# Backward of two linear-attention and two sliding-window layers: attention backward in 24 visits a chunk, weights transposed on TensorE, a set order for the forward's DMA queue, and later clearing of the ring

## The chip, the cores and the metric

The kernel runs on one core of a Trainium2 chip. TensorE (PE; its weight loads are shown apart as PEld), VectorE (DVE), ScalarE (ACT), GpSimd (POOL) and SyncE (SP, which only issues DMAs here) run side by side, each through its own instructions in order, and meet at semaphores. TensorE writes to PSUM alone, which has eight banks of 2 KB a partition. The metric is the time of one launch on the device in microseconds. Before: 2201.24 us, the median of three runs (2200.07 to 2201.99).

## The reference

Four residual blocks are applied to a sequence of 2048 rows of 640 columns in bfloat16: linear attention (weights A), sliding-window attention (weights B), then both once more with the same weights. The kernel returns the output, the gradient of the input, and the gradients of the four weight matrices, each summed over the two layers that share it.

```python
def _A_ref(x, wqkv, wo):                       # 32 heads of 20
    q, k, v = split(x @ wqkv)
    phi = lambda t: jnp.where(t > 0, t + 1, jnp.exp(t)) + 1e-6
    pq, pk = phi(q), phi(k)
    kv = jnp.einsum("bhsd,bhse->bhde", pk, v)
    z = jnp.einsum("bhsd->bhd", pk)
    o = jnp.einsum("bhqd,bhde->bhqe", pq, kv) / (jnp.einsum("bhqd,bhd->bhq", pq, z)[..., None] + 1e-6)
    return merge(o) @ wo
def _B_ref(x, wqkv, wo):                       # a window of 256 keys, causal
    q, k, v = split(x @ wqkv)
    scores = jnp.einsum("bhqd,bhkd->bhqk", q, k) * (20 ** -0.5)
    mask = (i - j >= 0) & (i - j < 256)
    p = softmax(jnp.where(mask, scores, -1e9))
    return merge(jnp.einsum("bhqk,bhkd->bhqd", p, v)) @ wo
x = x + _A_ref(layernorm(x), Aw, Ao);  x = x + _B_ref(layernorm(x), Bw, Bo)
x = x + _A_ref(layernorm(x), Aw, Ao);  x = x + _B_ref(layernorm(x), Bw, Bo)
_out, _vjp = jax.vjp(_f, A_x, A_wqkv, A_wo, B_wqkv, B_wo); grads = _vjp(grad_out)
```

With tiles of 128 rows there are 16 of them, and a window of 256 keys reaches over at most three tiles of keys: the query's own (masked on the diagonal), the one before it, and the one before that (masked the other way).

## The kernel before, in words

**Order of the work.** All is emitted by `passes` (L1268 on). (1) `forward`: a first pass over the 16 tiles for layer 0's features and their sums, then layers 0 and 1 together, tile by tile, then layers 2 and 3. (2) `core` for layer 3: the attention backward. (3) layer 2's linear backward. (4) `core` for layer 1. (5) layer 0's linear backward, with weight-gradient products between its steps, and then the rest of the weight gradients.

**Plans.** Each stage is a list of pairs (place, function). A place is a number of plan steps; the functions are emitted in the order of their places. The places stand in the table `PLACES` (L41). Four engines (PE, DVE, ACT, POOL) keep the order in which the code emits: `run` opens a `manual_schedule` with these four. The order of SP's queue, which issues every DMA, is left to a scheduler. `forward` has 430 plan steps before its end: the first pass has six steps a tile, the later layers eight (`B1`, `B3` are the first steps of the second and third part).

**Forward.** For a tile of layers 1 and 3, `qkv` writes q, k and v to a ring tile `s` (128 rows, 3 x 32 heads padded to 32 columns); two DMA transposes make its turned copy `T`; both are stored, 768 KB each, for the backward. The five ring tiles' padding is set at the very start, by three POOL memsets a tile (L284 to L286). `plan_scores` forms scores for four (head group, key tile) blocks in one visit: 16 matmuls on 32 rows, one `exp` of 128 x 2048 on ACT, masks on POOL; `b_pv` applies them to the values. Layer norm's reciprocal root is a POOL power (L424).

**Attention backward (`core`, `core_steps`, `core_step`, `core_acc`).** A chunk `c` is two query tiles. It is taken in four quarters of eight heads (two groups of four); each quarter loads its slabs (`core_loads`): q, k, v turned, and q and k as they are, for k and v over all four key tiles. A visit is one group, one query tile and two of the four heads: 32 visits a chunk. The visits are pipelined. In the step of visit n, PE forms the gradient scores `dp` of visit n-3 and the scores `s` of visit n (32-row matmuls on four row groups, one PSUM buffer of two banks for each), ACT makes `e = exp(s)`, DVE the product `ds = dp * e`, POOL masks `e`, and `ds` of an earlier visit is turned to `dsT`. Then comes a piece of the plan (norm backward, projections of the neighbouring chunks), and `core_acc` sums visit n-7 into two banks: 128 x 128 matmuls of 20 columns, from `ds`, `e` and `dsT`.

`dsT` is made in one of two ways. From the third chunk on, `by_dma` (table `bd`) sends 13 of 32 visits to a DMA transpose; the others are transposed by PE (L700) and copied by ACT (L705) or DVE (L707). Which of the two copies, and how many filler transposes PE gets (`thin`; six and four a visit in the first two chunks), is worked out by a small model of the engines' loads in `core`, corrected by table `xx`. After each group the banks are emptied: L753 keeps half of one for the next chunk, L757 adds that half, L759 scales the query gradient.

**Weights.** The backward needs each weight turned. `core`'s hooks of layer 3 load them by seven DMA transposes (`turned`), Wo of B is turned on PE near the end of the forward (`turn_wo`), and two are parked in memory for layer 1.

## Time and profile before

The profile shows one execution on the chip; the sequencers' own waits and issues are not counted as busy.

| what | value |
|---|---|
| median of the runs | 2201.24 us |
| the profiled execution, its span | 2199.58 us, 2197.9 us |
| granted TensorE clock, mean | 0.984 |
| busy: PE, DVE, ACT, POOL | 93 %, 63 %, 61 %, 49 % |
| DMA | 453.26 MB in 708193 packets, mean 206 GB/s |
| first and last `ds` of layer 3's backward | 659.8 us and 1091 us |
| first and last `ds` of layer 1's backward | 1261 us and 1690.7 us |

A row of the groups reads: line, engine, operation, what is written and from what, its shape, the count, then busy time and mean length of one in ns, then the idle time of the engine before it and what ended most of it. Matmuls overlap and their ends are modelled, so a matmul's length is longer than the distance from one to the next; that distance is told by the starts.

### The profile page before, as it was taken

The page shows a single profiled execution, that of the slowest core. Times are in us where ns is not written, and L with a number is a line of the kernel's source. Part 1 is how long each engine was busy: PE and PEld are TensorE (multiplying, and loading weights), DVE is VectorE, ACT ScalarE, POOL GpSimd, SP SyncE. Part 2 cuts the span into 40 slices and gives each one's busy share as a digit, 9 for nine tenths or more (in the row PEclk, how much of TensorE's full clock was granted, in tenths as well). Part 3 has the DMA queues.
Part 4 walks back from the last instruction along what each step waited for, and adds up shares of the span by engine and source line. Part 5 has one row for each costly group of instructions (what it writes and reads, how often), then busy time and mean ns, then how long its engine had stood idle before and what let it go on. Part 6 is the DMA issues. An engine that isn't in the chain of part 4 may idle for free. (4 is left out here: it accounts for less than half of the span.)

```text
span 2197.9 us, 74336 instructions
## 1 busy us (share of the span) xinstructions
PE 2041.3 (93%) x30981; PEld 1586.3 (72%) x30981; DVE 1390.2 (63%) x2840; ACT 1342.4 (61%) x2009; POOL 1083.0 (49%) x1887
## 2 busy tenths in 40 slices
PE   7989998899989999998879899999988899999999
PEld 5667776577767877777768687777776788888644
DVE  6788886888836887887748668888876233320000
ACT  5468886388876887887637677888876233330000
POOL 2046665166675577777534456777764312220000
PEclk9999999999999999999999999999999999999999
DMA  7498885799979499998799734999987999998650
GB/s 258 146 253 229 237 233 146 171 234 245 232 218 255 111 200 198 210 206 192 157 293 275 198 106 115 197 208 202 210 189 165 271 307 246 266 228 241 220 162 21
DMA packets 708193, 453.26 MB, mean 206 GB/s; under 512 B 419728, under 2 KB 684688, under 8 KB 707472
## 3 DMA queue, kind: packets, MB, share of 16 engines
q1 hardware_dynamic: 707856, 448.51, 81.2%
q8 instruction: 242, 3.96, 0.8%
q14 instruction: 95, 0.78, 0.1%
HBM read 213.09 MB, written 149.82 MB: 165 GB/s over the span
## 5 line engine op out<-in xcount | busy, mean ns | idle before, releaser
L680 DVE TENSOR_TENSOR ds<-dp,e 128x768 bf16<-128x768 f32 (+2 forms) x512 | 464.0, 906 | 173.8 <-PE s L138 55.6
L677 ACT ACTIVATE e<-s 128x768 bf16<-128x768 f32 (+2 forms) x512 | 395.7, 773 | 137.5 <-PE s L138 110.4
L383 ACT ACTIVATE eT<-sT 128x2048 bf16<-128x2048 f32 x180 | 338.0, 1878 | 89.0 <-PE sT L138 85.2
L138 PE MATMUL wg<-rhs,lhs 128*128 128x240 bf16 (+3 forms) x2880 | 372.2, 286 | 7.7 <-DMA lhs<-o 7.7
L138 PEld LDWEIGHTS <-lhs 128*128 128x128 bf16 x2880 | 262.1, 98 | 97.2 <-DMA lhs<-o 9.6
L689 POOL TENSOR_SCALAR_AFFINE_SELECT e<-e 128x256 bf16<-128x256 bf16 x512 | 207.2, 406 | 249.8 <-ACT e L677 246.9
L138 PEld LDWEIGHTS <-dqT 128*128 128x128 bf16 x1920 | 171.8, 98 | 62.2 <-issue 10.4
L391 POOL TENSOR_SCALAR_AFFINE_SELECT eT<-eT 128x512 bf16<-128x512 bf16 x256 | 165.5, 650 | 98.7 <-ACT eT L383 98.7
L138 PE MATMUL acc<-slabqs,ds 128*128 128x20 bf16 x2880 | 210.0, 172 | 1.4 <-ACT dq L759 0.5
L138 PE MATMUL dp<-slabvT,dT 32*128 32x384 bf16 (+2 forms) x1024 | 168.0, 320 | 44.3 <-DVE ds L680 39.6
L138 PE MATMUL acc<-ds,e 128*128 128x20 bf16 x2880 | 208.0, 171 | 0.0
L138 PEld LDWEIGHTS <-ds 128*128 128x128 bf16 x2880 | 187.9, 96 | 11.7 <-issue 3.5
L693 POOL TENSOR_SCALAR_AFFINE_SELECT e<-e 128x256 bf16<-128x256 bf16 x448 | 194.9, 435 | 0.0
L138 PEld LDWEIGHTS <-e 128*128 128x128 bf16 x2880 | 170.0, 96 | 10.6 <-issue 1.8
L1140 DVE CAST wr<-wg 128x240 bf16<-128x240 f32 (+3 forms) x54 | 24.4, 452 | 240.1 <-PE wg L138 228.8
L700 PE MATMUL flip<-ident,ds 128*128 128x128 bf16 x1944 | 169.7, 221 | 3.3 <-DVE ds L787 1.2
L138 PE MATMUL s<-slabkT,slabqT 32*128 32x384 bf16 (+2 forms) x1024 | 167.9, 323 | 4.1 <-ACT e L677 3.5
L1138 ACT CAST wr<-wg 128x240 bf16<-128x240 f32 (+3 forms) x36 | 14.3, 397 | 245.9 <-PE wg L138 241.3
L1033 POOL TENSOR_TENSOR dh<-dh,lg 128x640 f32<-128x640 f32 x32 | 46.0, 1437 | 238.1 <-DVE s L1030 235.1
L138 PE MATMUL dense<-WTA,dqT 128*128 128x320 bf16 x960 | 162.6, 301 | 0.6 <-DVE dqT L1007 0.3
L138 PE MATMUL dense<-WB,hnT 128*128 128x320 bf16 x960 | 160.1, 301 | 0.4 <-DVE s L500 0.3
L138 PE MATMUL acc<-slabks,dsT 128*128 128x20 bf16 x2880 | 147.3, 171 | 14.0 <-DMA dsT<-ds 13.0
(175 smaller groups left out, 4483.0 us busy)
## 6 DMA issues: line engine op xcount, KB each, us to landing
s<-s SPq DMA_DIRECT2D x32, 768.0 KB, 4.1
T<-T SPq DMA_DIRECT2D x32, 768.0 KB, 3.9
dqkv<-dq SPq DMA_DIRECT2D x16, 960.0 KB, 5.6
dqkv<-dqa SPq DMA_DIRECT2D x32, 480.0 KB, 5.1
rhs<-dqkv SPq DMA_DIRECT2D x32, 480.0 KB, 5.4
rhs<-dqkv SPq DMA_DIRECT2D x16, 960.0 KB, 6.5
slabkT<-T SPq DMA_DIRECT2D x56, 256.0 KB, 4.4
slabvT<-T SPq DMA_DIRECT2D x56, 256.0 KB, 3.9
```

Of the source, the lines that this page charges most:

```text
L138: return self.nc.tensor.matmul(out, lhsT=lhsT, rhs=rhs, start=start, stop=stop, skip_group_check=True, **kw)
L383: nc.scalar.activation(e, s, ACT.Exp)
L391: nc.gpsimd.affine_select(out=e, in_=e, compare_op=ALU.is_ge, fill=0.0, base=0, pattern=[[0, 4], [1, P]], channel_multiplier=-1)
L677: nc.scalar.activation(u.e[:, :, 0:u.cw], s[:, :, 0:u.cw], ACT.Exp)
L680: nc.vector.tensor_tensor(out=d.ds[:, :, 0:d.cw], in0=d.dp[:, :, 0:d.cw], in1=d.e[:, :, 0:d.cw], op=ALU.mult)
L689: nc.gpsimd.affine_select(out=dg, in_=dg, compare_op=ALU.is_ge, fill=0.0, base=0, pattern=[[0, 2], [-1, P]], channel_multiplier=1)
L693: nc.gpsimd.affine_select(out=fr, in_=fr, compare_op=ALU.is_ge, fill=0.0, base=-1, pattern=[[0, 2], [1, P]], channel_multiplier=-1)
L700: nc.tensor.transpose(ps[:, 3 * j + i, :], f.ds[:, j, i * P:(i + 1) * P], self.ident)
L1033: nc.gpsimd.tensor_tensor(out=x["dh"], in0=x["dh"], in1=L["g"][:, i, :], op=ALU.add)
L1138: nc.scalar.copy(o[:, 0:w], ps[:, 0:w])
L1140: nc.vector.tensor_copy(o[:, 0:w], ps[:, 0:w])
```

## The change

**Visits.** `core_visits` replaces `core_steps`: in each quarter and pair of heads, the twelve (group, query tile, key tile) blocks of two groups are split into three visits of four (two in chunk 0, where there are fewer keys). That is six visits a quarter and 24 a chunk. Neighbouring key tiles of one query tile form a run and share one matmul a head, unless they lie in different slabs. `e`, `ds` and `dsT` grow from 3 to 4 blocks a head, the lag from issue to `core_acc` falls from seven visits to six, two plan pieces go to each visit (one before and one after `core_acc`), and two masks at equal distance become one instruction. The load model is gone: copies, fillers and DMA visits stand in tables (`xx`, `th`, `bd`).

**Slabs.** k and v of two new tiles are loaded and those of the two older ones kept from the last chunk. The turned store is laid out as [row, quarter, q/k/v, 256] and written in three DMAs; only q and k of `s` are stored.

**Forward's DMA queue.** SP joins the manually ordered engines in `forward`; `put` holds a store or a transpose back by a number of plan steps (table `sp`) and `tick` lets it go.

**Weights.** `turn` transposes all four matrices on PE at plan steps 268 to 296, through the pool of `e`, and stores them; later stages `fetch` them.

**Ring clearing and start.** The memsets move to plan steps 21.7 to 50; 36 filler transposes stand at step 0.2; the first loads alternate with the first three weight loads. Places in `f1`, `f2`, `f3`, `s1`, `s3`, `bf` and `bh` are shifted by small amounts.

```diff
+    sp=[2.8, 2.1, 1, 0.6, 0.6, -2.1, 0.5, 0.7, 2, 1, 1, 0.7, 1, 1, 0.4, 0.5],
+    ms=[21.7, 29.5, 34.7, 42.1, 50.1],
+    th=[0, 2, 0, 4, 1, 1, 0, 1, 1, 2, 0, 2, 0, 1, 0, 3, 5, 1, 2, 1, 3, 0, 3, 1],
+    xx=[1, 0, 1, 1, 0, 1, 1, 1, 1, 1, 1, 1, 0, 1, 0, 1, 0, 1, 1, 1, 1, 0, 0, 1],
+    bd=[0, 1, 0, 0, 0, 0, 0, 1, 0, 1, 1, 0, 1, 1, 1, 0, 0, 1, 1, 1, 0, 1, 0, 0])
...
+    def put(self, kind, out, in_, transpose=False):
+        d = PLACES["sp"][kind]
+        if not self.spm or d <= 0:
+            self.dma(out, in_, transpose)
+        else:
+            self.queue.append((self.now + d, len(self.queue), out, in_, transpose))
+    def tick(self, n=1):
+        self.now += n
+        due = sorted((x for x in self.queue if x[0] <= self.now), key=lambda x: x[:2])
+        self.queue = [x for x in self.queue if x[0] > self.now]
+        for _, _, out, in_, transpose in due:
+            self.dma(out, in_, transpose)
...
+        def turn(w, dst, j, last, eng):
+            if j % 3 == 0:
+                stage["w"] = st.fpe.tile([P, 4 * 4 * P], BF, name="wT", tag="e")
+            tp = st.ps.tile([P, 8, P], BF, name="flip", tag="m")
+            for k in range(DT):
+                nc.tensor.transpose(tp[:, k, :], w[:, k, j * P:(j + 1) * P], self.ident)
+            o = stage["w"][:, j % 3 * D:(j % 3 + 1) * D]
+            if eng:
+                nc.scalar.copy(o, tp[:, 0:DT, :].rearrange("p a b -> p (a b)"))
+            else:
+                nc.vector.tensor_copy(o, tp[:, 0:DT, :].rearrange("p a b -> p (a b)"))
+            if j % 3 == 2 or j == last:
+                j0 = j - j % 3
+                self.put(15, dst[:, j0 * D:(j + 1) * D], stage["w"][:, 0:(j + 1 - j0) * D])
+        plan += [(a, lambda x=x, i=i: turn(*x, i % 4 != 3)) for i, (a, x) in enumerate(zip(PLACES["wt"], turns))]
...
-                self.dma(sv["s"][t], R["s"].rearrange("p a h d -> p a (h d)"))
-                self.dma(R["T"][:, 2], R["s"][:, 2].rearrange("p h d -> p (h d)"), transpose=True)
-                self.dma(sv["T"][t], R["T"].rearrange("p a g q -> p a (g q)"))
+                self.put(4, sv["s"][t], R["s"][:, 0:2].rearrange("p a h d -> p a (h d)"))
+                self.put(6, R["T"][:, 2], R["s"][:, 2].rearrange("p h d -> p (h d)"), transpose=True)
+                for j in range(3):
+                    self.put(4, sv["T"][t][:, :, j], R["T"][:, j].rearrange("p (c g) q -> p c (g q)", c=4))
...
+            order = [[(0, 0), (0, 1), (1, 1), (0, 2), (1, 2), (1, 3)], [(0, 0), (0, 1), (0, 2), (1, 2), (1, 3), (1, 1)]]
+            units = [(gi, bi, kk) for gi in range(2) for bi, kk in order[gi]]
+            m = len(units) // 3
...
+                u.by_dma = self.by_dma(24 * c + 6 * qr + 3 * p + v)
...
-        return n >= 64 and PLACES["bd"][n % 32] == 1
-    WARM = (6, 4)
+        return n >= 48 and PLACES["bd"][n % 24] == 1
+    WARM = (8, 5)
...
+            while x or y:
+                for z in (x, y):
+                    if z:
+                        z.pop(0)[1]()
+            u.e = st.pe.tile([P, 2, 4 * P], BF, name="e")
+            nc.scalar.activation(u.e[:, :, 0:w], s[:, :, 0:w], ACT.Exp)
+            nc.vector.tensor_tensor(out=d.ds[:, :, 0:w], in0=d.dp[:, :, 0:w], in1=d.e[:, :, 0:w], op=ALU.mult)
+            if d.by_dma:
+                self.put(14, d.dsT, d.ds.rearrange("p j k -> p (j k)"), transpose=True)
...
-                nc.vector.tensor_tensor(out=kv(old), in0=av(st.acc[0]),
-                                        in1=st.part[:, (G * c + g + 1) % (G + 1), :].rearrange("p (b w x) -> p b w x", b=2, w=2), op=ALU.add)
+                for b in range(2):
+                    nc.vector.tensor_tensor(out=cols(old, 1, 2)[:, b], in0=acc(st.acc[0])[:, b],
+                                            in1=acc(st.part[:, (n + 1) % (G + 1), :])[:, b], op=ALU.add)
...
-        st.lag = 7
+        st.lag = 6
...
-            for c in range(3):
-                hooks[8 + 5 * c] = lambda c=c: self.turned(st.WTB, "A", c)
-                hooks[36 + 5 * c] = lambda c=c: self.turned(st.WTB, "B", c)
-            hooks[52] = lambda: self.turned(st.WoTA, "A")
+            hooks[20] = lambda: self.fetch(st.WTB, self.WT["B"])
+            hooks[40] = lambda: self.fetch(st.WoTA, self.WoT["A"])
...
-        with self.tc.manual_schedule(engines={E.PE, E.DVE, E.Activation, E.Pool}):
-            self.passes()
+        with self.tc.manual_schedule(engines={E.PE, E.DVE, E.Activation, E.Pool, E.SP}):
+            next(g)
+            self.tick(99)
+        self.spm = False
+        with self.tc.manual_schedule(engines={E.PE, E.DVE, E.Activation, E.Pool}):
+            for _ in g:
+                pass
```

More of the change, by code (lines that the diff above doesn't have):

```diff
@@ L326, in forward @@
         plan += [(END - 32, begin_core), (END - 6, begin_slabs)]
[L328 to L333 removed]
+        plan.append((END - 31.5, lambda: self.fetch(st.core.WoT, self.WoT["B"])))
         first_ = {}
@@ L725, in prod @@
                 self.after(ins, st.accf[k])
-        for i in reversed(range(u.nb)):
-            kt = u.w0 + u.kk + i
+        for i in reversed(range(u.m)):
+            gi, bi, kk = u.blocks[i]
+            kt = u.w0 + kk
             k = 0 if kt < t0 else 1
```

395 lines of the change are left out of this document (230 added, 165 removed).

## The prediction

> **What bounds the kernel now.** I read the stages first (busy time by windows), then the groups and waits of one steady stretch of the attention backward, then single visits in order of time. All sums are made against one profiled execution:
>
> ```profile
> span 2197.9 us, 74336 instructions
> PE 2041.3 (93%) x30981; PEld 1586.3 (72%) x30981; DVE 1390.2 (63%) x2840; ACT 1342.4 (61%) x2009; POOL 1083.0 (49%) x1887
> ```
>
> Its own time is 2199.58 us, 1.7 above its span and 1.7 under the median of the runs, 2201.24.
>
> Windows: stretch, its length, then busy time of PE, PEld, DVE, ACT, POOL, granted clock, DMA share and GB/s.
>
> ```profile
> 0.00:12.40 12.40, 0.71 (x5) 0.45 (x5) 2.81 (x9) 1.98 (x2) 9.51 (x29) 1.00 0.87 286
> 30.00:85.00 55.00, 55.00 (x482) 42.01 (x481) 46.46 (x151) 37.45 (x83) 6.04 (x12) 1.00 0.53 180
> 200.00:300.00 100.00, 100.00 (x1802) 76.08 (x1800) 88.77 (x234) 84.44 (x72) 64.83 (x108) 1.00 0.85 231
> 360.00:410.00 50.00, 39.57 (x390) 26.16 (x389) 35.93 (x96) 17.06 (x27) 8.83 (x15) 0.89 0.27 85
> 824.00:1046.00 222.00, 202.73 (x3865) 162.04 (x3864) 175.25 (x259) 175.73 (x295) 164.94 (x321) 0.99 0.98 200
> 1690.80:2197.90 507.10, 487.05 (x4405) 372.61 (x4401) 106.52 (x258) 107.56 (x221) 70.20 (x50) 0.99 0.77 220
> ```
>
> The first 12.4 us hold almost no matmul; after that the first forward pass fills PE wholly, so a microsecond saved at the start is saved at the end. From 200 to 300, inside the first pair of forward layers, PE is full too. From 360 to 410, between the forward layer pairs, nothing is full. From 824 to 1046 (four chunks of an attention backward) PE, DVE, ACT and DMA are all near 80 to 98 per cent. The last 507 us, weight gradients, are PE's, and the change leaves them alone. How long the two attention backwards last is told by the product `ds` (L680) alone, 256 visits in each, the first 32 of them chunk 0:
>
> ```profile
> 659.70:703.30 43.60, 17.82 (x32) 0.94 1.04 243
> 703.30:1091.20 387.90, 213.28 (x224) 1.00 0.89 185
> 1261.30:1301.50 40.20, 17.84 (x32) 0.95 0.36 100
> 1301.50:1690.80 389.30, 213.34 (x224) 0.99 0.83 177
> ```
>
> Chunks 1 to 7 take 387.9/7 = 55.4 and 389.3/7 = 55.6 us, 1.73 us a visit. What sets this pace is seen in one visit (start, length) and in PE's waits of the steady stretch:
>
> ```profile
> 860.05 0.96 DVE L680 TENSOR_TENSOR ds<-dp,e 128x768 bf16<-128x768 f32 x1 [0.38 <-POOL gn L898]
> 861.06 0.34 PE L138 MATMUL dp<-slabvT,dT 32*128 32x384 bf16 x2 [0.21 <-DVE ds L680]
> 861.07 0.34 PE L138 MATMUL s<-slabkT,slabqT 32*128 32x384 bf16 x2
> 861.59 0.96 DVE L680 TENSOR_TENSOR ds<-dp,e 128x768 bf16<-128x768 f32 x1
> ...
> PE dp L138 <- DVE ds L680: 11.9, 29, 0.9
> PE acc L138 <- DMA dsT<-ds: 5.5, 5, 2.7
> ```
>
> There is one PSUM buffer for `dp`, so a loop runs DVE, PE, DVE: 0.96 for the product, 0.05 until `dp` starts, 0.53 until the next product starts. That is 1.54 us, and 32 x 1.54 = 49.3 of the 55.5. The other 6.2 us a chunk are visits in which another engine, or DVE's other work, is late. PE's largest wait is this loop (11.9 us), its next the DMA transposes (5.5).
>
> **The change part by part.** *Visits.* A chunk has 24 visits of four key blocks instead of 32 of three; the block products are the same in number. Rows of the steady stretch (824 to 1046), and below the line of dots three shapes from the whole run:
>
> ```profile
> L680 DVE TENSOR_TENSOR ds<-dp,e 128x768 bf16<-128x768 f32 x127 | 121.4, 956 | 43.0 <-PE s L138 13.8 <-ACT dsT L705 5.9 <-DMA dsT<-ds 5.6
> L707 DVE COPY dsT<-flip 128x768 bf16<-128x768 bf16 x32 | 17.5, 548 | 0.0
> L757 DVE TENSOR_TENSOR dq<-acc,part 128x320 bf16<-128x320 f32 x32 | 15.5, 485 | 3.4 <-PE acc L138 2.6
> L677 ACT ACTIVATE e<-s 128x768 bf16<-128x768 f32 x127 | 103.3, 813 | 34.9 <-PE s L138 29.8 <-POOL e L689 2.9 <-POOL ds L803 0.5
> L705 ACT COPY dsT<-flip 128x768 bf16<-128x768 bf16 x42 | 33.7, 803 | 0.1
> ...
> L680 DVE TENSOR_TENSOR ds<-dp,e 128x512 bf16<-128x512 f32 x32 | 22.1, 691 | 16.1 <-PE dp L138 10.0 <-POOL e L689 3.2 <-PE s L138 2.6
> L677 ACT ACTIVATE e<-s 128x512 bf16<-128x512 f32 x32 | 19.2, 602 | 4.0 <-PE s L138 3.8
> L812 ACT COPY dT<-flip 128x1024 bf16<-128x1024 bf16 x32 | 32.5, 1014 | 16.8 <-PE flip L811 16.8
> ```
>
> From 512 to 768 elements `ds` grows by 265 ns, so at 1024 it is 1.22 us: 24 x 1.22 = 29.3 a chunk for 30.6. `e` grows by 211, so 1.02: 24.6 for 26.0. Eleven of 24 visits are transposed by DMA (88 of 192 blocks) instead of 13 of 32 (78). Of the other 13, eleven `dsT` copies go to ACT and two to DVE. ACT: 11 x 1.01 = 11.2 for 42/4 x 0.80 = 8.4. DVE: two at about 0.67 (125 ns more per 256 elements than 0.55, an estimate) for eight at 0.55, 1.3 for 4.4. The add L757 becomes two halves, each about 0.32 by the `ds` slope: 5.2 for 3.9. DVE in all: -1.3 - 3.1 + 1.3 = -3.1 us a chunk; ACT -1.4 + 2.8 = +1.4, from 175.73/4 = 43.9 to 45.3. POOL's selects merge two into one in two visits of three; at 164.94 of 222 us POOL was the least busy of the four.
>
> PE makes 8 runs of `s` and `dp` per three visits in place of 4 per four, each with weights of its own. The forward's scores show such runs of 128 columns, four row groups at once:
>
> ```profile
> 250.13 0.23 PE L138 MATMUL sT<-T,T 32*128 32x128 bf16 x4
> 250.20 0.23 PE L138 MATMUL sT<-T 32*128 32x128 bf16 x4
> 250.26 0.28 PE L138 MATMUL sT<-T,T 32*128 32x128 bf16 x8
> ...
> L138 PEld LDWEIGHTS <-T 32*128 32x128 bf16 x2880 | 46.1, 93 | 46.3 <-issue 40.4 <-DMA T<-s 2.2
> ```
>
> A set of four follows the last after 0.06 to 0.07 us though a weight load lasts 0.093: the loads are hidden. So the loop grows only by one more set: 1.22 + 0.05 + 0.53 + 0.07 = 1.87 us, and 24 x 1.87 = 44.9 us in place of 49.3. If I keep the 6.2 us of lateness, a chunk takes 51.1. ACT at 45.3 would then be 89 per cent busy where it is 79 now, so I add 0.9: **52.0**, a gain of 3.5. Bounds: 55.5 (ACT eats it all) and 49 (the lateness falls with the visits too). Chunks 0 and 1 have all transposes on PE and eight and five filler transposes a visit (six and four before); there PE's own work sets the pace, and I take 2 us each. Per core stage 6 x 3.5 + 2 + 2 = 25, for two **-50 us** (bounds 0 and -80).
>
> The Trainium skill, page "TensorE: Matmul & The Clock Gate", Part 3, The mechanism, says that a weight load overlaps running matmuls only when its row group differs. By that rule the extra runs of the same row group would each wait for their load. The forward's rows speak against it, as the 0.07 shows; its price here is a rival below.
>
> *Slab loads.* Keys and values of the older two tiles are kept, so a quarter loads 640 KB instead of 1024.
>
> ```profile
> slabkT<-T SPq DMA_DIRECT2D x16, 256.0 KB, 4.9
> dsT<-ds SPq DMA_TRANSPOSE x52, 3.8
> ```
>
> At 200 GB/s and a share of 0.98 the 1.5 MB less a chunk are some 7 us of queue time; against them stand 88 transposed blocks for 78, beside 30 of `dqT`. I price this at nothing by itself: DMA is not the loop, and what it frees covers the larger transposes. If that cover fails, the second rival holds.
>
> *Start.* The ring clearing leaves POOL's queue:
>
> ```profile
> 1.92 1.31 POOL L284 MEMSET s<- 128x1152 bf16 x1
> 4.33 0.15 DVE L423 TENSOR_SCALAR rs<-bmv 128x1 f32<-128x1 f32 x1
> 9.80 0.57 POOL L424 TENSOR_TENSOR rs<-rs,mhalf 128x1 f32<-128x1 f32 x1
> 12.41 2.85 PE L138 MATMUL dense<-WA,h2T 128*128 128x320 bf16 x10 [0.79 <-ACT h2T L165]
> ```
>
> The first norm's power stands behind five clearings until 9.80, though its input is ready at 4.48. Next late is the first weight load. I take -5 (bounds 0 and -7). The clearings, 1.31 us and two short ones each, later fall into a POOL that is busy 6 of 55 us, and between a norm's scaling (2.3) and its flip (7.1) lie almost five plan steps. The 36 filler transposes stand where PE has nothing.
>
> *Weights turned on TensorE.* 40 turns of five transposes, 30 ACT copies and 10 DVE copies, 14 stores (6.5 MB) at plan steps 268 to 296, which is the 360 to 410 window.
>
> ```profile
> L165 ACT COPY h2T<-flip 128x640 bf16<-128x640 bf16 x32 | 22.1, 690 | 10.2 <-PE flip L162 10.1
> L167 DVE COPY oT<-flip 128x640 bf16<-128x640 bf16 x32 | 15.6, 487 | 1.5 <-PE flip L162 0.4
> ```
>
> ACT gets 20.7 us into a window where it is busy for 17, DMA is at 0.27. PE's 200 transposes at the sets' 0.06 are 12 us, against 10 idle. DVE, nearest to full, gets 4.9. Bounds 0 and +17 (12 + 4.9 on the path); I take +3, part of DVE's share. Out go seven DMA transposes of weights beside the third layer's backward, whose chunk 0 takes 43.6 us against the other's 40.2: -3. Behind the turns on PE stand the flips and projections of the next layer pair's first tiles, and with them all of its attention.
>
> *Set order of the forward's DMA queue.* Its waits now (120 us of steady forward, SP's longest):
>
> ```profile
> SPq L108 <- DVE bst L417: 20.1, 7, 4.1
> SPq L108 <- DVE hn L429: 11.1, 7, 1.9
> ```
>
> SP already stands waiting in order for a quarter of the time while PE, by the 200 to 300 window, is full, so no order gains much; a bad one delays the transposes `T` behind a store. The new T store is in 512 B pieces, three issues for one. I take 0 (bounds -8 and +10).
>
> Sum: -50 - 5 + 3 - 3 = -55, so 2199.6 - 55 = 2144.6, and 1.7 more for the median: **2146 us**.
>
> **The rivals.**
> *ACT takes over as the bound.* ACT is the one engine that gets more work, `s` too has one buffer, and the 89 per cent leaves it little room. If chunks 2 to 7 stay at 55.5, 12 x 3.5 = 42 us are lost: 2188. Against it: its idle time (29.8 of 34.9 us) waits for `s`, which stands behind `dp` and so behind DVE.
> *Late DMA transposes: slower.* A transpose is one third larger; from `ds` to its use in `acc` there are three visits (6.5 us less 1.22) instead of four (6.9 less 0.96), against 3.8 us to land now, and SP's queue is shared. There are 6 x 11 x 2 = 132 such visits. From 0.42 us of stall in each the whole 55 us is gone; at 0.6 it is 79 us, and 2225. The five waits of up to 2.7 us now speak for it, the smaller slab loads against.
> *The lateness falls as well.* DVE has 3.1 us less a chunk; if chunks 2 to 7 come to 49, that is 12 x 3 = 36 more: 2110.
> *Weight loads are exposed.* 32 more sets a chunk x 0.093 = 3.0 us, x 14 chunks = 42: 2188. The forward's sets speak against it. The skill's rule named above would make it so.
>
> **How the numbers follow.** My forecast 0.55 (own range 2126 to 2168), ACT bound 0.15, lateness falls 0.15, late transposes 0.10, exposed loads 0.05. Range 2103 to 2194: it holds the first, nearly all of the 2188 and most of the 2110 cases. A measurement here tells 0.2 per cent (4.4 us). Slower is the late transposes and a tail of the 2188 cases, 0.12; same 0.03; faster 0.85.
>
> **What would show it.** `ds` at 1.22 us, 24 to a chunk; chunks of 52 us; PE's wait for `ds` per chunk smaller, ACT 88 per cent busy; first dense product near 7.5 us; the window between the layer pairs no more than 3 us longer; score sets still 0.07 apart. It is wrong if `acc` waits for `dsT` by DMA for over 0.4 us a visit, if `s` waits for ACT's `e` in most visits, or if the forward's SP queue makes PE wait for `T`.

## The result and the profile after

The changed kernel takes 2187.98 us (median of 13 runs, 2176.98 to 2193.73), the kernel before 2200.07 on the same chips (13 runs, 2191.78 to 2203.28). The ratio is 0.9944, 95% interval 0.9928 to 0.9961: faster by 12 us, where the forecast had 55. The profiled execution took 2187.47 us, its span is 2185.8.

Windows by stage, first of before, then of after: the forward up to the first `ds`, layer 3's attention backward, the linear backward between, layer 1's attention backward, the rest. Columns as in the prediction.

```profile
0.00:659.70 659.70, 606.46 (x9716) 450.40 (x9716) 507.37 (x1355) 463.25 (x447) 344.79 (x589) 0.98 0.81 217
659.70:1091.20 431.50, 398.94 (x7598) 321.60 (x7597) 334.48 (x504) 335.20 (x571) 296.12 (x595) 0.99 0.90 191
1091.20:1261.30 170.10, 151.25 (x1694) 120.87 (x1691) 108.45 (x225) 101.47 (x202) 75.19 (x63) 0.95 0.92 256
1261.30:1690.80 429.50, 397.60 (x7583) 320.86 (x7583) 333.38 (x501) 334.94 (x570) 296.66 (x593) 0.99 0.78 170
```

```profile
0.00:680.40 680.40, 629.38 (x9946) 465.31 (x9947) 522.02 (x1362) 482.93 (x477) 345.81 (x590) 0.97 0.77 212
680.40:1088.80 408.40, 379.68 (x8376) 304.24 (x8376) 306.15 (x435) 344.38 (x517) 276.67 (x482) 0.99 0.78 161
1088.80:1264.00 175.20, 154.92 (x1701) 123.44 (x1697) 109.04 (x227) 103.25 (x205) 73.73 (x62) 0.92 0.86 250
1264.00:1677.20 413.20, 382.25 (x8374) 306.66 (x8374) 306.57 (x434) 343.75 (x516) 276.44 (x481) 0.98 0.75 154
1677.20:2185.80 508.60, 490.31 (x4405) 373.40 (x4401) 104.92 (x260) 108.21 (x224) 68.35 (x48) 0.98 0.76 218
```

The two attention backwards gain 23.1 and 16.3 us. The forward gives 20.7 back, the stretch between 5.1, the last 1.5 (507.1 before): -39.4 + 27.3 = -12.1. So there are two questions: why the visits gave less than 50, and what the forward lost. After, the groups of four chunks (822 to 1037):

```profile
L764 DVE TENSOR_TENSOR ds<-dp,e 128x1024 bf16<-128x1024 f32 x96 | 117.3, 1222 | 36.1 <-PE s L166 20.6 <-ACT dT L912 5.1 <-POOL dh L1001 4.7
L760 ACT ACTIVATE e<-s 128x1024 bf16<-128x1024 f32 x96 | 100.0, 1041 | 19.6 <-PE s L166 18.6 <-POOL e L775 0.2
```

PE's waits in the same stretch (total, times, longest), and then one visit in order of time:

```profile
PE dp L166 <- DVE ds L764: 9.5, 17, 1.1
PE acc L166 <- DMA dsT<-ds: 2.3, 4, 1.2
```

```profile
859.82 1.21 DVE L764 TENSOR_TENSOR ds<-dp,e 128x1024 bf16<-128x1024 f32 x1
861.08 0.23 PE L166 MATMUL dp<-slabT,dT 32*128 32x128 bf16 x2 [1.02 <-DVE ds L764]
...
861.13 0.28 PE L166 MATMUL dp<-slabT,dT 32*128 32x256 bf16 x2
...
861.24 0.23 PE L166 MATMUL dp<-slabT,dT 32*128 32x128 bf16 x2
...
861.57 1.23 DVE L764 TENSOR_TENSOR ds<-dp,e 128x1024 bf16<-128x1024 f32 x1 [0.54 <-POOL dh L1001]
```

`ds` takes 1.22 us as forecast; `dp` starts 0.05 after it and the next `ds` 0.49 after that, which makes this visit shorter than the 1.87 us worked out; the sets of `dp` follow one another at 0.05 to 0.11 us. Over these four chunks a quarter of the visits start within 1.88 us of the one before, the middle one after 2.09. So the floor of the visit and the sets' spacing are right, and most visits are above the floor. `acc` waits for DMA in four of 96 visits, 2.3 us in all. No wait for ACT's `e` stands in PE's list for this stretch.

### The profile page after: what moved, and what is told of

It is laid out like the page before. It is cut to its first block, busy times and chain, and to the rows that moved or that the text cites. A ratio compares the mean times of both kernels' runs of the same rounds, so it can differ in the third digit from the quotient of the medians.

```text
span 2185.8 us, 77047 instructions
## 1 busy us (share of the span) xinstructions
PE 2036.5 (93%) x32786; PEld 1573.0 (72%) x32786; DVE 1348.7 (62%) x2715; ACT 1382.5 (63%) x1937; POOL 1041.0 (48%) x1663
## 5 line engine op out<-in xcount | busy, mean ns | idle before, releaser
L764 DVE TENSOR_TENSOR ds<-dp,e 128x1024 bf16<-128x1024 f32 (+1 forms) x384 | 443.9, 1156 | 165.1 <-PE s L166 83.6
L760 ACT ACTIVATE e<-s 128x1024 bf16<-128x1024 f32 (+1 forms) x384 | 380.0, 990 | 87.8 <-PE s L166 83.2
L779 POOL TENSOR_SCALAR_AFFINE_SELECT e<-e 128x256 bf16<-128x256 bf16 x512 | 201.5, 408 | 168.7 <-ACT e L760 139.1
L791 ACT COPY dsT<-flip 128x1024 bf16<-128x1024 bf16 (+1 forms) x200 | 192.1, 960 | 11.9 <-PE flip L786 10.9
L166 PE MATMUL acc<-slabqs,ds 128*128 128x20 bf16 x2880 | 194.4, 172 | 1.4 <-ACT dq L846 1.0
L166 PE MATMUL acc<-ds,e 128*128 128x20 bf16 x2880 | 192.5, 171 | 0.0
L166 PE MATMUL dp<-slabT,dT 32*128 32x128 bf16 (+1 forms) x1952 | 155.3, 246 | 36.6 <-DVE ds L764 30.8
L775 POOL TENSOR_SCALAR_AFFINE_SELECT e<-e 128x512 bf16<-128x512 bf16 x224 | 142.7, 637 | 58.2 <-ACT e L760 56.0
L166 PE MATMUL dense<-WTB,dqT 128*128 128x320 bf16 x960 | 156.4, 302 | 1.9 <-DMA dqT<-dq 1.9
L166 PE MATMUL s<-slabT,slabqT 32*128 32x128 bf16 (+1 forms) x1952 | 148.6, 247 | 6.4 <-ACT e L760 5.6
```

The lines of the kernel that those rows point to most:

```text
L166: return self.nc.tensor.matmul(out, lhsT=lhsT, rhs=rhs, start=start, stop=stop, skip_group_check=True, **kw)
L760: nc.scalar.activation(u.e[:, :, 0:w], s[:, :, 0:w], ACT.Exp)
L764: nc.vector.tensor_tensor(out=d.ds[:, :, 0:w], in0=d.dp[:, :, 0:w], in1=d.e[:, :, 0:w], op=ALU.mult)
L775: nc.gpsimd.affine_select(out=v, in_=v, pattern=[[0, 4], [1 if far else -1, P]], **kw)
L779: nc.gpsimd.affine_select(out=v, in_=v, pattern=[[0, 2], [1 if far else -1, P]], **kw)
L791: nc.scalar.copy(v(f.dsT), v(ps))
```

## The experiments

Base is the changed kernel unless another is named. The forward's stages are read off three things: the outer products of the first pass (`M`, 96 of them), the exponentials `eT` of the two attention layers (180, the first 90 of layer 1), and the first `ds` of layer 3's backward.

**1. The forward's weight loads early.**

```diff
-    ld=[40, 60, 64, 70, 80],
+    ld=[3.1, 3.2, 3.3, 16, 20],
```

> Edit: the changed kernel with the five loads of WoA, WB and WoB planned at steps 3.1, 3.2, 3.3, 16 and 20 in place of 40 to 80. Theory (the first pass lost its early start because these loads now fall between 23 and 61 us, in the middle of it): the last outer product of the first pass, at 90.0 us in the changed kernel, comes at about 85; the scores of layer 1 and everything behind them move by the same 4 to 5 us (first ds of layer 3's backward 680.5 to about 676), total about 2183. Rival (the pads on GpSimd or the new places hold the first pass): the last outer product stays within 1 us of 90.0 and the total does not move.

2189.67 us, ratio to before 0.9955 (0.9938 to 0.9972): no gain, and the last outer product came later, at 93.5. PE's waits from 6 to 92 us:

```profile
PE M L166 <- DVE pqk L631: 6.3, 1, 6.3
```

Loaded there, the weights hold the first pass up once, for 6.3 us (DVE waits 6.1 us for a tile of x, whose load SP issues behind that of WB), in place of several times between 40 and 60. Neither theory is decided by this: the end of the pass did move, but the wrong way.

**2. No turning between the layers.** `turn`'s 40 steps go, and the DMA transposes and `turn_wo` of before come back.

```diff
-        plan += [(a, lambda x=x, i=i: turn(*x, i % 4 != 3)) for i, (a, x) in enumerate(zip(PLACES["wt"], turns))]
-        plan.append((END - 31.5, lambda: self.fetch(st.core.WoT, self.WoT["B"])))
+        plan += [(END - 31.5 + 2 * j, lambda j=j: turn_wo(j)) for j in range(DT)]
...
-            hooks[20] = lambda: self.fetch(st.WTB, self.WT["B"])
-            hooks[40] = lambda: self.fetch(st.WoTA, self.WoT["A"])
+                    hooks[k + 5 * c] = lambda c=c, kind=kind: turned(st.WTB[:, c * DT:(c + 1) * DT, :], self.W[kind][:, c * D:(c + 1) * D])
+            hooks[16] = lambda: self.dma(self.WoT["B"], flat(st.core.WoT))
+            hooks[27] = lambda: self.dma(self.WT["A"], flat(st.WTB))
+            hooks[52] = lambda: turned(st.WoTA, self.Wo["A"])
```

> Edit: the changed kernel without the 40 weight-turning steps between the forward layers; the weights are turned as in the kernel before, by five transposes of WoB on TensorE at the end of the forward and by seven transposing DMAs in layer 3's backward. Theory (the turning steps lie one for one on TensorE's path): the scores of layer 3 come 9 to 12 us earlier (eT number 90 from 426.2 to about 416), the first ds of layer 3's backward from 680.5 to about 665 to 671, layer 3's backward gets 0 to 3 us longer, total about 2174 to 2180. Rival (the window waits for something else than the turning): eT number 90 stays within 3 us of 426.2 and the total within 3 us.

2177.74 us, ratio to before 0.9899 (0.9867 to 0.9931), 10 us under the changed kernel. The window between the layer pairs (from the 85th `eT` to the 91st) in before, after and this kernel:

```profile
353.60:415.20 61.60, 49.05 (x546) 33.55 (x543) 42.66 (x112) 23.69 (x34) 13.09 (x23) 0.89 0.36 111
```

```profile
354.90:426.30 71.40, 59.16 (x744) 43.78 (x741) 48.16 (x124) 43.00 (x64) 13.66 (x24) 0.98 0.60 197
```

```profile
356.40:414.60 58.20, 44.99 (x547) 31.60 (x544) 42.10 (x112) 23.80 (x35) 13.21 (x23) 0.97 0.45 130
```

The turning makes the window 13.2 us longer and PE's busy time in it 14.2; PE's idle time is 12.6, 12.2 and 13.2 us in the three, so the turning took next to none of it. Against that stands layer 3's backward, whose chunk 0 (`ds` alone, this kernel, then after) is 7.0 us longer:

```profile
666.70:710.50 43.80, 16.57 (x24) 0.90 1.00 237
```

```profile
680.40:717.20 36.80, 16.56 (x24) 1.00 0.36 118
```

In the kernel of this experiment three weight transposes fill the DMA queue there (SP in order of time), a slab load stands behind them, and PE waits for it, which is 3.4 of the 7.0 us; the rest is not taken apart, and the clock there is 0.90 for 1.00 (waits from 690 to 712):

```profile
688.49 11.74 SPq L115 DMA_TRANSPOSE WTB<-in_B_wqkv_dram  x3
```

```profile
PE s L166 <- DMA slabqT<-T: 3.4, 1, 3.4
```

**3. The forward's queue left to the scheduler.**

```diff
-        self.queue, self.now, self.spm = [], 0, True
+        self.queue, self.now, self.spm = [], 0, False
...
-        with self.tc.manual_schedule(engines={E.PE, E.DVE, E.Activation, E.Pool, E.SP}):
+        with self.tc.manual_schedule(engines={E.PE, E.DVE, E.Activation, E.Pool}):
```

> Edit: the changed kernel with the order of the forward's DMA queue left to the scheduler, as in the kernel before; nothing else. Theory (the forward's losses come from the turning, the late loads and the low clock, not from the set order of the queue): the first ds of layer 3's backward stays within 4 us of 680.5, except that the scheduler may pull the weight loads forward, which is worth up to 5 us at the end of the first pass. Rival (the set order is what costs the forward its 20 us): first ds at about 660 to 665, total about 2168.

2197.42 us, ratio to before 0.9993 (0.9971 to 1.0015): 9.4 us slower than the changed kernel. Both theories missed: for the changed kernel the set order is a gain. PE's first wait in the layers 2 and 3, in this kernel (429 to 598 us):

```profile
PE sT L166 <- DMA T<-s: 5.7, 7, 1.9
```

In the changed kernel no such wait is listed for the same steps (426 to 589). Over the whole run PE waits for `T` 12.2 us here, 4.1 in the changed kernel and 3.3 in the kernel before: by these waits the set order gains against a free order of the new stores, not against before. The turned store now goes out in three DMAs in place of one, and a free order lets the transposes `T` come late; that it is these stores that hold them was not tried.

**4. Wo of B turned at the end of the forward again**, nothing else.

```diff
-        plan.append((END - 31.5, lambda: self.fetch(st.core.WoT, self.WoT["B"])))
+        plan += [(END - 31.5 + 2 * j, lambda j=j: turn_wo(j)) for j in range(DT)]
```

> Edit: the changed kernel in which layer 3's backward again gets its WoB by 25 transposes on TensorE in the last steps of the forward (5.5 us of TensorE by 218 ns each) in place of a fetch. Theory (without these transposes TensorE idles and its clock falls in the last 50 us of the forward): the low-clock intervals between 620 and 675 us go, the last eT comes about 5 us earlier (669.3 to about 664), total 3 to 6 us less. Rival (the clock falls there for another reason, and the transposes are only more work): the low clock stays and the last eT comes 0 to 5 us later.

2185.31 us, ratio 0.9938 (0.9915 to 0.9961). The last `eT` came 2.6 us earlier (666.7) though PE has 5.5 us more to do, and the clock of the stretch to the first `ds` went from 0.87 to 0.92 only. Inconclusive: 2 us of total are inside what the runs of one kernel differ by, and 8 shows that the last `eT` moves by as much from one profile of the same steps to another.

**5. Loads in 25 pieces and pads at steps 99 to 111, on the base of 2.**

```diff
+        plan += [(24.5 + 3 * i, lambda x=x: part(*x)) for i, x in enumerate(parts)]
-    ms=[21.7, 29.5, 34.7, 42.1, 50.1],
+    ms=[99.5, 102.5, 105.5, 108.5, 111.5],
```

> Edit: the version without turning between the layers (the second experiment), with the weights of WoA, WB and WoB loaded in 25 pieces of one block of rows each, three steps apart from step 24 on, and with the pads of the rings cleared at steps 99 to 111 in place of 21 to 50. Theory (the first pass lost its early start in two places: to the slower normalisations, 798 in place of 446 ns, while GpSimd clears pads, and to stores that wait behind whole weight loads at 44 to 49 us): the last outer product of the first pass comes at 86 to 87 us in place of 90.0, everything behind it 3 to 4 us earlier, total about 2174. Rival (the pass is bound otherwise): 90 within 1 us, total within 3 us of 2177.7.

2178.61 us, ratio 0.9899 (0.9878 to 0.992); the last outer product at 89.8. It looks like the rival, and is not, as 9 shows: the pass, from its first outer product (12.4) to its last, takes 77.4 us, the changed kernel's 77.9, so the pads cost at the new place what they cost at the old. The norm `hn` beside a clearing in the changed kernel, at 18.6 us, and in experiment 5, at 77 us:

```profile
18.59 1.06 POOL L311 MEMSET s<- 128x1152 bf16 x1
18.68 1.15 DVE L477 TENSOR_SCALAR hn<-xi,bmv,rs 128x640 bf16<-128x640 bf16 x1 [0.67 <-POOL rs L472]
```

```profile
77.82 1.06 POOL L311 MEMSET s<- 128x1152 bf16 x1
77.91 1.15 DVE L484 TENSOR_SCALAR hn<-xi,bmv,rs 128x640 bf16<-128x640 bf16 x1 [0.67 <-POOL rs L479]
```

**6. Five more ACT copies a chunk to DVE, on the base of 2.**

```diff
-    xx=[1, 0, 1, 1, 0, 1, 1, 1, 1, 1, 1, 1, 0, 1, 0, 1, 0, 1, 1, 1, 1, 0, 0, 1],
+    xx=[1, 0, 0, 1, 0, 1, 0, 1, 1, 0, 1, 1, 0, 1, 0, 0, 0, 1, 1, 1, 0, 0, 0, 1],
```

> Edit: the version without turning between the layers, with 5 of the 11 ACT copies of transposed ds in each chunk given to DVE (ACT 6, DVE 7 of the 13 by TensorE). ACT falls by 5 x 1.03 = 5.2 us a chunk, DVE rises by 5 x 0.68 = 3.4. Theory (ACT, 85 % busy and waited for by the next scores, makes the visits late): chunks 2 to 7 fall from 53.0 to about 51 to 51.5 us, total 18 to 24 us less (about 2157). Rival (DVE's product ds is what comes late, and DVE now stands at 84 %): chunks 2 to 7 stay or rise by up to 1.5 us, total 0 to 18 us more.

2175.79 us, ratio 0.9888 (0.9867 to 0.9909), against 2177.74: no change. Chunks 2 to 7 of both backwards, this kernel:

```profile
756.10:1076.40 320.30, 292.62 (x6505) 231.80 (x6502) 261.73 (x381) 246.91 (x371) 224.97 (x380) 0.99 0.92 182
1343.10:1665.20 322.10, 296.40 (x6506) 234.17 (x6503) 261.72 (x381) 247.38 (x371) 224.88 (x380) 0.97 0.91 181
```

642.4/12 = 53.5 us a chunk, where experiment 2 has 53.3 (320.6 and 318.5). ACT has 23 us less to do in each stretch than in the changed kernel (270.7) and DVE 15 more, and the chunk does not show it. The 1.5 to 2 us a chunk that the theory promised from ACT's relief did not come. But the edit gives to one engine what it takes from the other, so a small gain and a small loss that cancel are not ruled out.

**7. The 24 visits behind the old forward**: the edits of 2 and 3, the tables `f1`, `f2`, `f3`, `s1` and `s3` of before, and

```diff
-    ms=[21.7, 29.5, 34.7, 42.1, 50.1],
+    ms=[0, 0, 0, 0, 0],
...
-        plan += [(0.2, lambda: self.warm(36, st.ps.tile([P, 8, P], BF, name="warm", tag="m")))]
```

> Edit: the visits of 24 a chunk behind a forward like that of the kernel before: no turning between the layers, the DMA queue's order left to the scheduler, the places of the forward's steps as they were, pads cleared at the start, no filler transposes at the start. Theory (apart from the turning, the forward's other edits gain and lose about the same): first ds of layer 3's backward within 4 us of the second experiment's 666.8, total about 2174 to 2182. Rival (the set order and the new places are worth the 10 us by which the third experiment was slower): first ds at 672 to 680, total about 2185 to 2192.

2185.32 us, ratio 0.993 (0.9909 to 0.9951), first `ds` at 669.5. Between the two: the rival's 2185 is met by the total, the theory's 4 us by the first `ds`. The first product comes 5.4 us later here than in the changed kernel (12.4 for 7.0), and the first pass ends at the same 90.0.

**8. GpSimd's first folds and splits at the end of the forward given to DVE, on the base of 2.**

```diff
-                first_.update(enumerate(self.slots(self.plan_before(st, 3, 0, st.core, ((1, 2, 3, 4.5, 10), (2, 4, 5, 10, 12))), 16)))
+                first_.update(enumerate(self.slots(self.plan_before(st, 3, 0, st.core, ((1, 2, 3, 4.5, 10), (2, 4, 5, 10, 12)), quick=True), 16)))
```

> Edit: the version without turning between the layers, with GpSimd's folds and splits of the first tile of layer 3's preparation (about 3.3 us in the forward's last steps) given to DVE. Theory (TensorE's gap of 2.8 us behind GpSimd there, against 1.8 before, and the low clock that follows it are two to three of the microseconds that the end of the forward lost): the gap falls under 1 us, the last eT comes 2 to 4 us earlier against the scores before it (78.7 us from eT number 150 to the last, to about 75), total 2 to 4 us less. Rival (the end is bound by ACT's eT): 78.7 stays within 1 us.

**2172.77 us, ratio to before 0.9877 (0.9855 to 0.9899)**: the lowest median of the kernels here that compute the reference, 15 us under the changed one and 27 under before. The last `eT` moved from 655.9 to 651.9. The end of the forward (from the 151st `eT` to the first `ds`) in before, after and this kernel:

```profile
577.80:659.70 81.90, 70.60 (x1401) 54.57 (x1399) 43.36 (x108) 63.48 (x43) 60.04 (x103) 0.99 0.82 227
```

```profile
589.00:680.40 91.40, 77.82 (x1395) 57.23 (x1393) 42.63 (x105) 64.33 (x43) 60.88 (x104) 0.87 0.82 224
```

```profile
577.20:664.00 86.80, 74.05 (x1420) 56.16 (x1419) 46.17 (x116) 64.42 (x44) 57.68 (x99) 0.96 0.88 224
```

After has as many PE instructions there as before and 7.2 us more of PE's time, at a granted clock of 0.87 for 0.99. PE's longest wait for GpSimd there went from 2.8 us to 1.9, not under 1. What that is worth is not shown: one and the same forward differs as much from profile to profile. From the 151st `eT` to the last, the base took 78.7 us in experiment 2 and 75.6 in 6, whose forwards are the same; with this edit it took 74.8 here and 76.6, 74.6 and 77.8 in 10, 12 and 13. The clock of 0.96 is of this run too (0.93 in 10, on the same steps), and the runs of 6 (2172.14 to 2179.02) and 8 (2169.85 to 2175.47) overlap.

**9. Pads cleared by DVE at the very start, loads in pieces, on the base of 8.**

```diff
-            nc.gpsimd.memset(R["s"][:, :, :, DH:HP], 0.0)
+            nc.vector.memset(R["s"][:, :, :, DH:HP], 0.0)
```

> Edit: the version without turning and with the folds on DVE (the experiment before, 2172.8 us), in which the pads of the five rings are cleared by DVE at the very start, where it waits for the first load, and the forward's weights are loaded in 25 pieces. Theory (clearing on GpSimd during the first pass slows DVE's normalisations and takes back about 1.1 us of the early start per ring, wherever it is put in the pass): tiles of the first pass 4.74 us each from the first to the last, the last outer product at 85 to 86 us in place of 90, total about 2168. Rival (the last outer product is held at 90 us by something else, as it stood there in four kernels): 89 to 90 and no gain.

The outer products of the first pass in before, after and this kernel (median length, first and last start):

```profile
L138 PE MATMUL M<-va,pqk x96: 216/218/222, 17.9 to 89.6; 128*120 128x126 bf16 x96
```

```profile
L166 PE MATMUL M<-va,pqk x96: 215/218/267, 12.1 to 90.0; 128*120 128x126 bf16 x96
```

```profile
L166 PE MATMUL M<-va,pqk x96: 215/218/266, 15.6 to 87.1; 128*120 128x126 bf16 x96
```

The pass takes 71.7 us before, 77.9 after and 71.5 here: without GpSimd's clearing and the large loads in its midst it runs at its old pace. DVE's clearing holds the start up by 3.5 us instead. The pass begins 2.3 us earlier than before and ends 2.5 earlier, 2.9 under the changed kernel and not the 4 to 5 expected: what is left of the early start is kept. The total, 2177.07 (0.9882, 0.9851 to 0.9912), does not show them: 4 runs each, and the end of the forward went at a lower clock again (0.91 from 575 to 661 us).

**10 and 12. No fillers in the visits; two more in each of 13 visits, on the base of 8.** First 10, then 12:

```diff
-    th=[0, 2, 0, 4, 1, 1, 0, 1, 1, 2, 0, 2, 0, 1, 0, 3, 5, 1, 2, 1, 3, 0, 3, 1],
+    th=[0] * 24,
...
+    th=[2, 4, 2, 6, 3, 3, 2, 3, 3, 4, 2, 4, 2, 3, 2, 5, 7, 3, 4, 3, 5, 2, 5, 3],
```

> Edit: the same base (2172.8 us) without the 16 filler transposes a chunk in the visits from chunk 2 on: TensorE has 16 x 0.057 = 0.9 us less to do in each chunk. Theory (a visit is late because TensorE, 92 % busy, is in the middle of other work when ds ends): chunks 2 to 7 fall by 0.5 to 0.9 us from about 53.2, total 6 to 11 us less. Rival (the fillers stand in time that TensorE waits anyway, and without them its clock falls more often): chunks the same or up to 1 us longer, more low clock, total 0 to 12 us more.

> Edit: the same base with two more fillers in each of the 13 visits of a chunk whose ds is transposed on TensorE: 26 x 0.057 = 1.5 us more of TensorE a chunk. Theory (TensorE's own work makes the visits late): chunks 2 to 7 rise by 0.8 to 1.5 us, total 8 to 18 us more. Rival (TensorE has the time, and the fillers keep its clock up): chunks within 0.5 us, low clock less, total 0 to 6 us less.

**11. WB alone turned in the last 30 steps of the forward, on the base of 8**; WA and WoA come by DMA as in 2.

```diff
+            nc.vector.tensor_copy(stage["w"][:, j % 3 * D:(j % 3 + 1) * D], tp[:, 0:DT, :].rearrange("p a b -> p (a b)"))
...
+        plan += [(401 + 1.5 * j, lambda j=j: turn(WB, self.WT["B"], j, NF - 1)) for j in range(NF)]
...
+            hooks[36] = lambda: self.fetch(st.WTB, self.WT["B"])
```

> Edit: the same base, but the 15 blocks of WB are turned on TensorE in the last 30 steps of the forward (16.5 us of TensorE by 15 x 5 x 0.219, copies on DVE) in place of between the layers or by DMA; WA and WoA are turned by DMA in layer 3's backward. Theory (turning costs one for one where TensorE is full, as between the layers, and little in the last 50 us of the forward, where TensorE waits for ACT 6 to 8 us and runs at a low clock): the last eT comes 2 to 8 us later, the first chunk of layer 3's backward falls from 44 to 37 to 41 us because three of its seven DMA transposes are gone from the queue of its slab loads, total between -5 and +3 us against 2172.8. Rival (it costs its full 16 us there too): last eT 14 to 17 us later, total about 2182.

2187.41 us, ratio to before 0.9927 (0.9905 to 0.9949). The last `eT` came at 667.5 for 651.9 in 8, 15.6 us later, and chunk 0 of layer 3's backward gained 6.7 (38.1 for 44.8). The rival's time for `eT` is met, but by luck: its 16.5 us add up the lengths of 75 transposes, which overlap, and their busy time is 7.2 us. The other half are waits. PE's waits for `eT` in this stretch rose from 6.3 us to 13.4, and it waits 2.0 us for a copy `wT`. ACT's `eT` waits 19.3 us for PE's `ops`, which read the `eT` before; in 8 no such wait is listed. The tiles `wT` come from the pool of `e`, and two of the copies wait 6.7 us for a store of `wT`, so a shortage of these buffers is the likely cause; that was not tried.

**13. Fewer products for dq, on the base of 8.** This kernel leaves out two thirds of the products of dq, so its gradients are not the reference's.

```diff
+                if (gi, bi, u.p, j) in st.seen:
+                    continue
+                st.seen.add((gi, bi, u.p, j))
                 prod(0, 320 + 80 * bi + (2 * gi + j) * DH, u.dsT[:, 4 * j + i, :], ...)
```

> Edit: the version without turning and with the folds on DVE (2172.8 us); of the 192 products of a chunk that add up dq (acc from slabks and dsT), only the first of each block of queries and head is made, 64, so that dq is not the reference's; everything else is done. TensorE has 128 products a chunk less, 3.5 us at 27 ns from one product to the next, 5.6 at the 43 ns of the group's busy time (31.6 us for 728). Theory (what makes a visit late is TensorE being in the middle of other work when ds ends; 1.5 us more of it made chunks 1.0 longer): chunks 2 to 7 fall from 53.0 to 49.5 to 51 us, total 24 to 42 us less. Rival (the loop from dp over ds to the next dp, with its latencies, and the clock set the chunk): chunks within 0.7 us of 53.0, total within 8 us.

Chunks 2 to 7 of both backwards in 8, 10, 12 and 13, a fence each:

```profile
759.60:1080.40 320.80, 296.51 (x6513) 234.04 (x6512) 246.57 (x351) 270.49 (x401) 225.30 (x381) 0.98 0.91 182
1344.20:1661.90 317.70, 293.42 (x6513) 232.25 (x6512) 246.75 (x351) 270.16 (x401) 225.29 (x381) 0.99 0.92 183
```

```profile
763.50:1083.60 320.10, 294.00 (x6412) 228.75 (x6409) 247.01 (x351) 269.53 (x400) 225.17 (x380) 0.98 0.94 182
1346.50:1670.40 323.90, 297.31 (x6413) 230.88 (x6412) 246.95 (x351) 270.48 (x401) 225.30 (x381) 0.96 0.92 179
```

```profile
758.60:1085.00 326.40, 301.64 (x6655) 241.28 (x6655) 247.94 (x351) 270.85 (x401) 225.57 (x381) 0.98 0.91 179
1351.70:1675.50 323.80, 298.96 (x6659) 239.53 (x6659) 247.06 (x351) 270.25 (x402) 225.42 (x381) 0.99 0.91 180
```

```profile
759.80:1074.30 314.50, 279.58 (x5745) 216.06 (x5742) 244.28 (x351) 268.87 (x400) 228.06 (x380) 0.98 0.91 185
1338.80:1653.50 314.70, 280.04 (x5745) 216.14 (x5744) 243.65 (x351) 269.62 (x401) 228.30 (x381) 0.98 0.92 185
```

Twelfths of the two lengths: 53.2, 53.7, 54.2 and 52.4 us a chunk. Totals: 2178.03 without fillers (0.9892, 0.9864 to 0.9919), 2188.73 with more (0.9936, 0.9911 to 0.9962), 2159.94 with fewer products (0.9804, 0.9781 to 0.9826). More PE work costs two thirds of what it takes, 1.0 of 1.5 us. Less of it hardly pays: without fillers PE's busy time does not fall (591.3 us in both stretches for 589.9; in the second the granted clock is 0.96 for 0.99, in the first, at 0.98 in both, it falls by 2.5 us and the length by 0.7); with 2.5 us of busy time a chunk less, the chunk falls by 0.8. Neither theory of 13 holds as put: the chunk stays within the rival's 0.7 us of 53.0, the total falls by 12.8 where it allowed 8, and PE's work gives back about a third of its own size.

## Why the prediction was wrong

The direction and the range were right, the size was not: of 55 us forecast 12 came. That the range holds the result is luck: it reached so far up for two rivals at 2188, ACT as the bound and exposed weight loads, and neither came about.

*Visits, -50: measured -39.4, of which 7.0 belong to the DMA transposes (experiment 2), so some -32.* The floor is as worked out. Chunks 0 and 1 gained 11 us where 8 were taken, but 6.8 of them in chunk 0 of layer 3, where the DMA transposes went; the visits gave some 4 there. Chunks 2 to 7, six to a stage, took (stretches before, then after):

```profile
756.50:1092.10 335.60, 306.86 (x5862) 245.25 (x5859) 266.02 (x390) 263.94 (x441) 243.53 (x475) 0.99 0.94 191
1354.70:1691.70 337.00, 308.04 (x5862) 245.70 (x5859) 265.83 (x390) 264.18 (x441) 244.62 (x475) 0.99 0.90 189
```

```profile
768.30:1089.40 321.10, 296.35 (x6513) 233.16 (x6512) 246.40 (x351) 270.73 (x401) 225.87 (x381) 0.98 0.91 181
1354.50:1677.70 323.20, 297.16 (x6513) 234.38 (x6512) 246.84 (x351) 270.61 (x402) 226.03 (x381) 0.98 0.90 180
```

That is 56.05 and 53.69 us a chunk, a gain of 2.4 where 3.5 was taken (the prediction's 55.5 is the mean of chunks 1 to 7). The step that failed is "if I keep the 6.2 us of lateness": the lateness grew. 53.7 less the floor of 44.9 leaves 8.8, against 56.05 less 49.3, 6.8, before. The starts in the two traces say where it sits. From the end of `ds` to the first `dp` it is 0.05 us in the loop; the mean over these chunks is 0.25 before and 0.34 after, which makes 32 x 0.20 = 6.3 us a chunk before and 24 x 0.29 = 7.0 after. From the first `dp` to the next `ds` the mean is 0.68 after, 0.08 above the loop, another 1.9 us (0.8 before). After, `dp` starts more than 0.1 us after the end of `ds` in 157 of 286 visits, and in each of them PE comes straight from other work: 95 times from `dense`, the plan piece that now stands behind `core_acc`, 62 times from `acc` (before, 185 of 382, all from `acc`). The visit that follows the one shown above, whose `ds` ends at 862.80, is such a one:

```profile
862.64 0.84 PE L166 MATMUL dense<-WoTA,gT 128*128 128x320 bf16 x5
863.41 0.28 PE L166 MATMUL dp<-slabT,dT 32*128 32x256 bf16 x2
```

I added up DVE and ACT by chunk and not PE, whose busy time fell only from 51.2 to 49.5 us a chunk while the loop fell from 49.3 to 44.9; so PE's own work, done in its order, more often outlasts a `ds` (in 55 per cent of the visits for 48). It is no plain bound: by experiment 13 less of it gives back a third only, and how much a better order would give was not tried. ACT, on which I had laid the extra 0.9, is 84 per cent busy, not 88, and PE lists no wait for `e`; the first rival, ACT as the bound, falls with that and with 56.05 to 53.69. Late transposes fell too (2.3 us in four chunks), and so did exposed weight loads: the sets stand 0.05 to 0.11 apart. The Trainium skill, page "TensorE: Matmul & The Clock Gate", Part 3, The mechanism, has a sentence by which a load overlaps running matmuls only where the row group differs; it would have exposed them, and these rows disagree with it. The same section also lets a load go ahead into a background weight buffer, which these rows do not contradict.

*Weights turned, +3: measured +9.8 against before, +13.2 by experiment 2.* After the visits this is the largest error of a term. I set PE's 12 us "against 10 idle". The 200 transposes take 16.6 us of PE's busy time, and idle time in a window is not room: PE stood idle there 12.6 us before and 12.2 after. Its waits before are for results of DVE and ACT, none longer than 1.6 us; that each is the latency of a chain in order, between whose links the turns did not fall, is how I read it and was not tried. The upper bound, 17, was nearer. Experiment 11 is no second case of the same: there half of the price is waits.

*DMA transposes gone, -3: measured -7.0 in chunk 0* (experiment 2): 3.4 of it is the wait for the slab load behind them, which the rows of before could not show.

*Start, -5: measured -5.4 at the first product and 0.4 late at the end of the first pass.* "The clearings later fall into a POOL that is busy 6 of 55 us" looked at the wrong engine: POOL had the time, but DVE, 84 per cent busy, is held while POOL clears (experiments 5 and 9).

*Set order, 0: about 0 against before, by PE's waits for `T` (4.1 us for 3.3).* But "no order gains much" is wrong for the changed kernel, which a free order makes 9.4 us slower (experiment 3): I did not ask what the three stores for one, which I had noted, would do in it.

*Left out of the sum:* the end of the forward, +9.5 us at a lower granted clock (the same steps took 88.5 us in experiment 1 and 88.8 in 4 for 91.4, so about 3 of it are of this one profile), and the stretch between the two backwards, +5.1, where the clock went from 0.95 to 0.92 with 3.7 us more of PE's busy time for the same instructions. Part of the order in these stages is the new split of steps at the begin and end of the visits; I did not separate it.

Sum: -39.4 - 0 + 9.8 + 9.5 + 5.1 + 1.5, and 1.4 elsewhere in the forward, is -12.1. The DMA transposes are inside the first term, the set order inside the forward's.

## What to carry to other kernels

Work put on a busy in-order engine "in its idle time" should be priced in full unless the trace shows what the engine waits for at that place and that the work fits into that wait. A start made earlier is worth something only if the rest of the stage keeps its pace: follow the gain by milestones to the stage's end, and ask of each moved instruction which other engine it holds up. On an engine that takes turns with another in a loop, ask where in the visit each piece of its work stands: taking work away gave back a third of its length here. And before an edit is credited with a few microseconds of one stretch, see how far two profiles of the same code differ there; here it was 3.

## What was not expected of the hardware

*GpSimd's clearing holds DVE.* `hn` takes 1.15 us beside a clearing of 1.06 and 0.446 without one (before, 20 to 40 us, four of them: the mean):

```profile
L429 DVE TENSOR_SCALAR hn<-xi,bmv,rs 128x640 bf16<-128x640 bf16 x4 | 1.8, 446 | 1.2 <-POOL rs L424 1.2
```

They meet because `hn` waits for GpSimd's power and the clearing is next in GpSimd's queue: from 10 to 60 us each of the four clearings has an `hn` of 1.15 us starting 0.09 us behind it, and the other five take 0.45. The Trainium skill, page "SBUF — State Buffer", section "SBUF: two separate sides", says that DVE in its two-port modes and GpSimd hold a shared port pair one at a time, for a whole instruction. The 1.15 for 0.446 agrees, and so does the pass's pace in experiment 9. In which mode `hn` runs the trace does not say, and it ends 0.18 us after the clearing, sooner than a whole `hn` started behind it would.

*The granted clock can fall after short gaps.* Busy time after, from 620 to 640 us, and before, at the same place of the forward; then PE's waits after, from 600 to 640:

```profile
620.00:640.00 20.00, 16.32 (x302) 11.83 (x301) 7.19 (x17) 14.93 (x9) 12.31 (x21) 0.81 0.79 216
```

```profile
608.80:628.80 20.00, 15.94 (x343) 12.33 (x340) 8.63 (x21) 15.91 (x10) 13.76 (x23) 1.00 0.87 245
```

```profile
PE sT L166 <- ACT eT L428: 5.0, 7, 1.0
PE sT L166 <- DMA T<-s: 1.4, 1, 1.4
```

The longest wait is 1.4 us, and the clock is 0.81. Such gaps do not always do it: before, PE is busy 15.9 of the 20 us and waits up to 1.8 us for GpSimd between 600 and 650, and the clock there is 1.00. What decides between the two is open. The Trainium skill, page "TensorE: Matmul & The Clock Gate", section "Why this matters for your kernels", warns of idle gaps over some 3 us; here gaps of 1.0 to 1.4 us went before a fall. The 13 runs of the changed kernel go with the clock: 2176.98 and 2178.06 us at 0.982, 2190.51 and 2193.73 at 0.972, about 1.5 us for each thousandth between these ends. That the low clock causes the time, and not the same waits both, is not shown by this.
